# A spectral filter and an MLP mixer on one core: fixed places in the six channel pairs for the length-47 steps and the token quarters, and intermediate writes on SyncE's queue

## The chip, the core and the metric

The kernel runs on one core of one Trainium2 chip. The metric is the time of one execution in device microseconds (us); the median of several runs is quoted. A core has TensorE (PE: matmuls, with PEld for its weight loads), VectorE (DVE), ScalarE (ACT), GpSimd (POOL) and SyncE (SP), which here does nothing but issue transfers. All data are float32.

## The reference

```python
# x: (8, 3008, 256), filt_r and filt_i: (1505, 256)
X = np.fft.rfft(x, axis=1)
y = np.fft.irfft(X * (filt_r + 1j * filt_i)[None], n=3008, axis=1)
# the mixer on y: w_tok1 (3008, 256), w_tok2 (256, 3008), w_ch1 (256, 1536), w_ch2 (1536, 256)
yt = y.transpose(0, 2, 1)
h = np.maximum(yt @ w_tok1, 0.0) @ w_tok2
u = y + h.transpose(0, 2, 1)
out = u + np.maximum(u @ w_ch1, 0.0) @ w_ch2
```

## The kernel before

**The filter.** A sequence of 3008 = 47 x 64 is transformed in two stages. The steps **a** are the length-64 stage: one matmul of a sample's loaded rows (L472), a copy by ScalarE into a tile `t1` (L478, two buffers) and a write to a DRAM buffer `z` (L479), 12 a steps for a sample. The length-47 stage has 16 rounds c for a group of samples, each with three steps:

- **b** (`b_pair`): four pairs of matmuls into the two banks "acc" and "b" (L572), which VectorE then multiplies with the filter's rows into `p1` and `p2` (L583, two products of 128x1024 where the group has two samples)
- **m** (`join`): a subtraction and an addition on VectorE (L588, L589)
- **i** (`bi_pair`): matmuls into the same two banks (L572), two copies by ScalarE to `t3` (L561), and two writes to a DRAM buffer `g` (L598)

After b of round c, SP loads what round c+2 needs: two parts of `z` (L532), a table (L493) and eight pieces of the filter (L206, L208). Before the first b there is a step **w**, in which the first two rounds' loads are issued.

The samples stand in groups: (0), (1, 2), (3, 4), (5, 6), (7). Sample 0 is filtered ahead of everything. Each other group's filter runs in small steps beside the mixer of the group before it: samples 1 and 2 (the first transform here) beside the mixer of sample 0, 3 and 4 (the second) beside that of 1 and 2, 5 and 6 (the third) beside that of 3 and 4, and 7 (the fourth, half as wide) beside that of 5 and 6.

**The mixer.** The token product makes `u` in six tiles m of 512 columns (the last has 448) for each sample; the channel product goes through each tile in six **pairs** jp of hidden channels. Both products of the samples from 1 on use seven block products in place of eight, with sums on VectorE. A pair is issued in this order by `mix`, which hands over at three **places**:

- `up_first`: four matmul groups (L783) into two banks "pg", a copy `s` by ScalarE (L786), then on VectorE one `hh` and one `s` (L761). Then the sums `t` of the pair before (three pieces, L761) and the first part of `down` for the pair before (three groups, L817). *Place 0.*
- `up_last`: three groups (L799) into the same "pg" banks, two additions to `hh` on VectorE and two relus on ScalarE (L804). *Place 1.*
- the second part of `down` for the pair before (four groups, L817); in pair 0 this ends the tile before. *Place 2.*

`one_step` takes one piece of VectorE work from a list: after a tile's end those of `finish` (two at place 2 of pair 0, then one each at the next places: ten VectorE pieces, the last two being the transposes `turn`), after the next tile's `u` those of `u_sums` (a first piece, then two). Stores of a tile go out on POOL's queue (L864).

The next tile's `u` is made by `u_parts` at places that the table `own` gives. Sample 0 has two units (`u_unit`, L690 and L682). The other samples have four **quarters** (`u_quarter`, L704, quarters 2 and 3 also L682), each in one of the banks "acc" and "b", emptied by VectorE (quarter 0 by ScalarE and VectorE). After a quarter's last, SP loads the next token weights (`w2m_load`, L723). In pair 2 of a sample's last tile stand the next sample's token sums (L660, 96 matmuls). So a, b, i, the token units, the quarters and the token sums share two banks.

At every place the last loop looks whether the coming step of the filter is due there; only the order of instructions on each engine is set by this, and every engine works through its own in that order, held by semaphores. Before, for the groups from the second transform on:

```python
if coming in "aw":
    due = group == 0 or place == 1
elif group:
    due = (i % 2, place) == {"b": (1, 1), "m": (0, 0), "i": (0, 2)}[coming]
```

Of the kernel before, what the change touches and what calls it, by code (L numbers as in the profile page):

```python
# [27 lines left out]
KH = KR // 2  # L28
HALF = 64
XC = 2  # L30
# [5 lines left out]
KC = 2  # L36
# [5 lines left out]
JP = JT // 2  # L42
# [10 lines left out]
GROUPS = ((0,), (1, 2), (3, 4), (5, 6), (7,))  # L53
# [59 lines left out]
def kernel(  # L113
# [11 lines left out]
    nc = tc.nc  # L125
# [11 lines left out]
    place_of = {b: (g, i) for g, bs in enumerate(GROUPS) for i, b in enumerate(bs)}  # L137
    z_d, g_d = ([nc.dram_tensor("%s_tmp%d" % (what, g), (K2, KR, len(bs), D), FP32, kind="Internal").ap()
                 for g, bs in enumerate(GROUPS)] for what in "zg")
# [25 lines left out]
    def bank(tag):  # L165
        return (psg if tag == "pg" else psum).tile([P, 512], FP32, tag=tag, name="ps_" + tag)
# [5 lines left out]
    def free_bank():  # L172
        turn.reverse()
        return turn[0]
# [227 lines left out]
    def convert():  # L402

        convert_middle()
        convert_end()
# [60 lines left out]
    def rows_of(t_d, b):  # L466
        g, i = place_of[b]
        return t_d[g].rearrange("k (g a) b d -> (k g) a b d", a=A)[:, :, i, :]

    def a_unit(b, c):  # L470
        ps = bank(free_bank())
        nc.tensor.matmul(ps, wa0 if b == 0 else wa, xs.pop((b, c)).rearrange("p a d -> p (a d)"), start=True, stop=True)  # L472
        if b == 0:
            d0, c = divmod(c, NXC // 2)
            nc.scalar.copy(out=turned[:, ts(c, 2 * XC), ds(d0 * P, P)], in_=ps.rearrange("p (a d) -> p a d", d=P))
            return
        t1 = t1p.tile([P, XC, D], FP32, tag="t1", name="t1")
        nc.scalar.copy(out=t1.rearrange("p a d -> p (a d)"), in_=ps)  # L478
        nc.scalar.dma_start(rows_of(z_d, b)[:, ts(c, XC), :], t1)  # L479

    def dft(bs):
        first = bs[0] == 0
# [77 lines left out]
        def by_block(out, ps):  # L560
            nc.scalar.copy(out=out.rearrange("p b (e g i) -> p b g e i", e=DH, i=CW),  # L561
                           in_=ps.rearrange("p b (g e i) -> p b g e i", e=DH, i=CW))

        def two_banks():
            return [bank(tag).rearrange("p (b d) -> p b d", b=2)[:, 0:nb, :] for tag in turn]
# [3 lines left out]
        def four(outs, stat, mov):  # L569
            for i in range(2):  # L570
                for j in range(2):
                    nc.tensor.matmul(outs(i, j), stat(i, j), mov(i, j), start=True, stop=True)  # L572

        def both(half, n=HALF):
            return slice(half * HALF, half * HALF + n)
# [15 lines left out]
        def bi_pair(c):  # L591
            pss, wb, p = two_banks(), wbs[c], prods.pop((c, 0))
            four(lambda i, h: pss[i][both(h)], lambda i, h: wb[both(i), 2 + h], lambda i, h: p[both(i), h])
            t3 = t3p.tile([P, KC, nb, D], FP32, tag="t3", name="t3")
            for i in range(KC):
                by_block(t3[:, i], pss[i])
            for h in range(2):
                nc.scalar.dma_start(g_d[place_of[bs[0]][0]][ts(c, KC), ts(h, KH)].rearrange("k r b d -> r k b d"),  # L598
                                    t3[both(h, KH)])

        for c in range(FB):
# [49 lines left out]
    def t4_load(b, c, lo=PARTS[0], hi=P, queue=nc.sync):  # L651
        if lo == 0:
            t4[b, c] = t4p.tile([P, TC4, D], FP32, tag="t4", name="t4")
        queue.dma_start(t4[b, c][lo:hi], rows_of(g_d, b)[lo:hi, ts(c, TC4), :])
# [238 lines left out]
    def mix(next_ready):  # L893

        wait = []
        pos, hhs, tts = {}, {}, {}

        def loads(b):
            if b + 1 < B and next_ready(b):
                for c in wait:  # L900
                    t4_load(b + 1, c)
                wait.clear()


        own = ({(4, 0): (0,), (4, 2): (1,)}, {(3, 0): (0, 1), (4, 0): (2, 3)})
        new = {(JP - 2, 0): (0, 1), (JP - 1, 0): (2, 3)}

        def u_parts(b, m, jp, place):
            parts = own[b > 0] if m + 1 < MT else new if b + 1 < B else {}
            now = parts.get((jp, place), ())  # L910
            b, m = (b, m + 1) if m + 1 < MT else (b + 1, 0)
            for part in now:
                u_part(b, m, part)
            if now and now[-1] == max(p for ps in parts.values() for p in ps):
                if m:
                    wait.append(m)
                todo_v.extend(v_steps(b, m))
                if b and (b, m) < (B - 1, MT - 2):
                    w2m_load((m + 2) % MT)

        to_dram = [f for m in range(MT) for f in w2_sums(m)]
        items = [(b, m, jp) for b in range(B) for m in range(MT) for jp in range(JP)]
        n = MT * JP
        for i in range(len(items) + 1):
            now, old = i < len(items), i >= 1
            if ended[0] < len(tiles):
                convert()
            if now:
                b, m, jp = items[i]
                if i % n == 0:  # L930
                    wait.append(0)
                w = width(m)
                hhs[i] = hp.tile([P, 4, 256], FP32, tag="hh", name="hh")
                g = [bank("pg").rearrange("p (s n) -> p s n", s=2) for _ in range(2)]
                s = up_first(jp, uts[b, m], vts[b, m], w, g)
                up_middle(hhs[i], w, g, s)
            one_step()
            if old:
                bo, mo, jo = items[i - 1]
                tts[i - 1] = tp.tile([P, 4, 256], FP32, tag="t", name="t")  # L940
                for f in h_sums(hhs[i - 1], tts[i - 1], width(mo)):
                    f()
                down(mo, jo, 0, hhs[i - 1], tts[i - 1], pos.setdefault((bo, mo), []))
            if now:
                u_parts(b, m, jp, 0)
            yield b, i % n, 0
            if ended[0] < len(tiles):
                convert()
            if now:
                up_last(jp, uts[b, m], vts[b, m], w, g, s, hhs[i])  # L950
            one_step()
            loads(b)
            yield b, i % n, 1
            if old:
                down(mo, jo, 1, hhs.pop(i - 1), tts.pop(i - 1), pos[bo, mo])
                if jo == JP - 1:
                    todo_v.extend(finish(bo, mo, uts[bo, mo], pos[bo, mo]))
                    one_step()
                    one_step()
            if now:  # L960
                if b + 1 < B and i % n == n - 4:
                    h1s[b + 1] = token_relu(b + 1, token_sums(b + 1))
                u_parts(b, m, jp, 2)
                if jp == JP - 1:
                    while todo_v and m + 1 == MT:
                        one_step()
                if i >= 8 and to_dram:
                    to_dram.pop(0)()
                if i in (28, 29):
                    w2m_load(i - 28)  # L970
            loads(b)
            yield b, i % n, 2
        while todo_v:
            one_step()

    with tc.manual_schedule():
# [6 lines left out]
        for i, _ in enumerate(dft(GROUPS[0])):  # L983
            if i == 0:
                nc.scalar.dma_start(wai_t, wait_d)
            k = i - NXC - 2
# [50 lines left out]
        group, todo, done = -1, iter(()), True  # L1037

        def next_ready(b):
            return done or b != GROUPS[group][-1]  # L1040
# [3 lines left out]
        coming = "a"  # L1044
        for b, i, place in mix(next_ready):
            if group + 1 < len(GROUPS) and b == GROUPS[group + 1][0]:
                if not done:
                    raise AssertionError("the filter's steps don't fit beside the mixer's")
                group += 1
                done = group + 1 == len(GROUPS)  # L1050
                todo = iter(()) if done else dft(GROUPS[group + 1]) if group else second
                coming = "a"
            if done:
                continue
            if coming in "aw":
                due = group == 0 or place == 1
            elif group:
                due = (i % 2, place) == {"b": (1, 1), "m": (0, 0), "i": (0, 2)}[coming]
            elif i < 27:
                due = (i % 3, place) in {"b": ((2, 1), (0, 2)), "m": ((0, 0), (1, 1)), "i": ((0, 1), (2, 0))}[coming]  # L1060
            else:
                due = place == {"b": 2, "m": 0, "i": 1}[coming]
            if due:
                coming = next(todo, "end")
                done = coming == "end"
# [30 lines left out]
```

## Time and profile before

| | |
|---|---|
| median of three runs | 2552.43 us (2550.9 to 2552.93) |
| the profiled execution's own time | 2553.45 us |
| its span, first to last instruction | 2551.7 us |
| granted TensorE clock, mean | 0.993 |
| busy: PE, PEld, DVE | 2444.5, 1984.0, 1811.3 us |
| busy: ACT, POOL | 675.5, 595.5 us |
| moved by DMA | 235.96 MB, 92 GB/s over the span |

The difference between an execution's time and its span is what lies before the first and after the last instruction. A line of the profile's groups or of the order of time names the engine, the line in the kernel, the operation and the tiles written and read; an "issue" or "q" behind an engine's name (SPq, ACTq) is its own queue of instructions, which issues transfers. Matmuls are pipelined, and their ends in the trace are modelled, so what a matmul costs is read from start to start.

### The profile page before, as it was taken

What the parts mean: (1) busy time and instruction counts of PE and PEld (TensorE: products, weight loads), DVE (VectorE), ACT (ScalarE), POOL (GpSimd) and SP (SyncE); (2) the same over time, 40 slices, a digit from 0 to 9 for tenths busy, and PEclk for the clock granted to TensorE, in tenths of its full rate; (3) what the DMA queues carried; (4) which work ended last, traced back from release to release, by engine and by line L of the source; (5) the groups of instructions that cost most, each with busy time, mean ns of one, the idle gap of its engine ahead of it and who ended that gap; (6) DMA issues with size and microseconds to landing.
All of it is one profiled execution on the core that took longest, in us unless ns stands there. A gap on an engine that the chain in (4) does not pass through costs nothing.

```text
span 2551.7 us, 33219 instructions
## 1 busy us (share of the span) xinstructions
PE 2444.5 (96%) x11716; PEld 1984.0 (78%) x11716; DVE 1811.3 (71%) x3344; ACT 675.5 (26%) x1348; POOL 595.5 (23%) x1086
## 2 busy tenths in 40 slices
PE   6889999999999999999999999999999999999997
PEld 3556666788877777888887777798888888898887
DVE  6686777576685887756775788757778577757776
ACT  4633222123221222222222222212222122212221
POOL 6573332112111121221121111211211121211222
PEclk8999999999999999999999999999999999999999
DMA  9974444243342333224333333314232222101100
GB/s 202 242 217 127 115 123 139 72 127 107 101 107 65 89 98 80 69 76 124 95 96 80 91 93 80 85 31 127 87 99 78 57 61 71 55 25 30 42 14 19
DMA packets 172478, 235.96 MB, mean 92 GB/s; under 512 B 32386, under 2 KB 122742, under 8 KB 172312
## 3 DMA queue, kind: packets, MB, share of 16 engines
q1 hardware_dynamic: 98728, 137.77, 19.3%
q0 software_dynamic: 33376, 48.46, 7.7%
q10 hardware_dynamic: 40208, 47.61, 6.4%
q8 instruction: 93, 1.52, 0.3%
q14 instruction: 73, 0.60, 0.1%
HBM read 156.49 MB, written 77.22 MB: 92 GB/s over the span
## 4 chain that ended last, share of the span: by engine, by line
PE 74%; DVE 13%; DMA 5%; ACT 3%; issue 3%; ACTq 1%; POOL 0%; DVEq 0%; SPq 0%; POOLq 0%
PE ps_po L817 27%; PE ps_pg L783 15%; PE ps_pg L799 11%; PE ps_b L660 3%; PE ps_acc L660 3%; DVE t L761 3%; PE ps_b L572 3%; PE ps_acc L704 3%; DVE hh L761 2%; PE ps_b L704 2%; DVE p L583 2%; DVE s L761 2%; PE ps_b L682 2%; PE ps_acc L682 2%; PE ps_b L472 1%
## 5 line engine op out<-in xcount | busy, mean ns | idle before, releaser
L761 DVE TENSOR_TENSOR hh<-ps_pg,s 128x512 f32<-128x512 f32 (+3 forms) x864 | 483.0, 587 | 493.2 <-ACT s L786 481.6
L864 POOL DMA_DIRECT2D out_dram<-r x757 | 410.5, 551 | 1679.2 <-ACT hh L804 805.3
L804 ACT ACTIVATE hh<-hh 128x512 f32<-128x512 f32 (+1 forms) x576 | 347.5, 621 | 1204.7 <-DVE hh L761 1204.7
L817 PE MATMUL ps_po<-t,wc 128*128 128x256 f32 (+1 forms) x2304 | 546.6, 380 | 12.8 <-DVE t L761 11.6
L817 PEld LDWEIGHTS ps_po<-t,wc 128*128 128x128 f32 x2304 | 429.7, 190 | 146.8 <-issue 42.9
L783 PE MATMUL ps_pg<-v,wc 128*128 128x256 f32 (+1 forms) x1728 | 415.3, 376 | 2.2 <-DVE v L761 2.1
L817 PE MATMUL ps_po<-hh,wc 128*128 128x256 f32 (+1 forms) x1728 | 414.1, 376 | 0.4 <-DVE r L761 0.2
L783 PEld LDWEIGHTS ps_pg<-v,wc 128*128 128x128 f32 x1728 | 328.7, 191 | 42.8 <-DVE v L761 4.8
L817 PEld LDWEIGHTS ps_po<-hh,wc 128*128 128x128 f32 x1728 | 329.3, 191 | 38.8 <-DVE r L761 0.6
L799 PE MATMUL ps_pg<-u,wc 128*128 128x256 f32 (+1 forms) x1152 | 294.2, 378 | 14.2 <-DVE hh L761 14.1
L799 PEld LDWEIGHTS ps_pg<-u,wc 128*128 128x128 f32 x1152 | 214.9, 190 | 56.5 <-DVE hh L761 26.0
L761 DVE TENSOR_TENSOR t<-t,hh 128x256 f32<-128x256 f32 (+1 forms) x576 | 243.7, 423 | 19.8
L761 DVE TENSOR_TENSOR s<-ps_pg,hh 128x512 f32<-128x512 f32 (+1 forms) x288 | 196.1, 681 | 30.3 <-DVE hh L761 0.5
L761 DVE TENSOR_TENSOR t<-hh 128x512 f32<-128x512 f32 (+1 forms) x288 | 192.6, 669 | 0.6 <-ACT hh L804 0.6
L783 PE MATMUL ps_pg<-u,wc 128*128 128x256 f32 (+1 forms) x576 | 175.9, 387 | 9.4 <-DVE hh L761 9.4
L786 ACT COPY s<-ps_pg 128x256 f32<-128x256 f32 (+1 forms) x288 | 105.9, 368 | 248.8 <-PE ps_pg L783 238.6
L799 PE MATMUL ps_pg<-v,wc 128*128 128x256 f32 (+1 forms) x576 | 168.7, 375 | 0.0
L783 PEld LDWEIGHTS ps_pg<-u,wc 128*128 128x128 f32 x576 | 104.7, 191 | 63.9 <-DVE hh L761 30.8
L799 PEld LDWEIGHTS ps_pg<-v,wc 128*128 128x128 f32 x576 | 108.6, 190 | 13.2
L583 DVE TENSOR_TENSOR p<-ps_b,filt 128x1024 f32<-128x1024 f32 (+1 forms) x64 | 69.4, 1084 | 24.3 <-PE ps_acc L572 20.0
L761 DVE TENSOR_TENSOR u<-ps_acc,u 128x512 f32<-128x512 f32 (+2 forms) x108 | 62.4, 578 | 31.8 <-PE ps_acc L704 27.1
L660 PE MATMUL ps_b<-t,w 128*128 128x256 f32 x384 | 83.6, 379 | 0.7 <-issue 0.7
(135 smaller groups left out, 2420.0 us busy)
## 6 DMA issues: line engine op xcount, KB each, us to landing
w<-w_tmp SPq DMA_DIRECT2D x35, 896.0 KB
out_dram<-r POOLq DMA_DIRECT2D x698, 32.0 KB, 1.8
g_tmp<-t ACTq DMA_DIRECT2D x112, 192.0 KB
z_tmp<-t ACTq DMA_DIRECT2D x84, 256.0 KB
t<-g_tmp SPq DMA_DIRECT2D x42, 512.0 KB
filt<-in_x_dram SPq DMA_DIRECT2D x145, 128.0 KB
t<-z_tmp SPq DMA_DIRECT2D x96, 192.0 KB
wb<-wbi_t SPq DMA_DIRECT2D x64, 128.0 KB
```

Source lines behind the costliest of these rows:

```text
L572: nc.tensor.matmul(outs(i, j), stat(i, j), mov(i, j), start=True, stop=True)
L583: nc.vector.tensor_tensor(out=prods[c, h], in0=pss[h].unsqueeze(1).to_broadcast([P, 2, nb, D]), in1=filts[c % FB][:, :, 0, :].unsqueeze(2) ...
L660: nc.tensor.matmul(acc[:, t, :], w1[:, a, ts(t, P)], t4[b, a // TC4][:, a % TC4, :], start=(a == 0 and t == 0), stop=(a == A - 1 and t == ...
L682: nc.tensor.matmul(ps[:, ds(q * P, n)], t4[b, c][:, r, ts(dh, P)], wai[:, 0:n], start=(first and q == 0), stop=(not first and q == 3))
L704: nc.tensor.matmul(ps[:, ds(j * hw, hw)], h1[:, n, :], w2m[m % 2][:, at, 0:hw], start=(i < 2 and j == 0), stop=(j == len(todo) - 1))
L761: nc.vector.tensor_tensor(out=out, in0=in0, in1=in1, op=op)
L783: nc.tensor.matmul(ps[:, 0:hw], chan[0][:, jp, n, :], mov, start=True, stop=True)
L786: nc.scalar.copy(out=s[:, 0], in_=g[0][:, 0, 0:hw])
L799: nc.tensor.matmul(ps[:, 0:hw], chan[0][:, jp, n, :], mov, start=True, stop=True)
L804: nc.scalar.activation(out=hs, in_=hs, func=AF.Relu)
L817: nc.tensor.matmul(po[i][:, j, 0:hw], chan[1][:, jp, n, :], mov, start=(jp == 0 and first == 1), stop=(jp == JP - 1 and last == 1))
L864: q.dma_start(bass.AP(tensor=ob.tensor, offset=ob.offset + row * D + g * cw, ap=[[N1 * D, 32], [D if h else -D, n], [1, cw]]), blocks[ts(g ...
```

## The change

- From the second transform on, b, m and i get fixed places in the six pairs of a tile, two rounds in a tile: b at place 1 of pairs 5 and 2, m at place 0 of pairs 0 and 3, i at place 0 of pair 1 and place 2 of pair 3. Before, a round began in every second pair, so three in a tile.
- In the first transform, b stands at place 1, m at place 2 and i at place 0 of the next pair; rounds begin in pairs 5, 1, 2 and 3, from tile 4 on in pair 0 too.
- From the second transform on, a and w steps come at places 1 and 2 of a pair, not at place 1 alone.
- The quarters 0 to 3 stand at place 0 of pair 3, place 0 of pair 4, and place 2 of pair 4 (two), not in two twos at place 0 of pairs 3 and 4. Sample 0's two units stand both at place 2 of pair 4, not one at place 0. For a sample's first tile (`new`) nothing is changed.
- The writes of `g` in `bi_pair`, and those of `z` from samples 3 on, are issued by SyncE, not by ScalarE.

```diff
@@ a_unit
-        nc.scalar.dma_start(rows_of(z_d, b)[:, ts(c, XC), :], t1)
+        (nc.scalar if b in GROUPS[1] else nc.sync).dma_start(rows_of(z_d, b)[:, ts(c, XC), :], t1)
@@ bi_pair
-                nc.scalar.dma_start(g_d[place_of[bs[0]][0]][ts(c, KC), ts(h, KH)].rearrange("k r b d -> r k b d"),
+                nc.sync.dma_start(g_d[place_of[bs[0]][0]][ts(c, KC), ts(h, KH)].rearrange("k r b d -> r k b d"),
                                     t3[both(h, KH)])
@@ mix
-        own = ({(4, 0): (0,), (4, 2): (1,)}, {(3, 0): (0, 1), (4, 0): (2, 3)})
+        own = ({(4, 2): (0, 1)}, {(3, 0): (0,), (4, 0): (1,), (4, 2): (2, 3)})
         new = {(JP - 2, 0): (0, 1), (JP - 1, 0): (2, 3)}
@@ the last loop
+            jp = i % JP
             if coming in "aw":
-                due = group == 0 or place == 1
+                due = group == 0 or place > 0
             elif group:
-                due = (i % 2, place) == {"b": (1, 1), "m": (0, 0), "i": (0, 2)}[coming]
-            elif i < 27:
-                due = (i % 3, place) in {"b": ((2, 1), (0, 2)), "m": ((0, 0), (1, 1)), "i": ((0, 1), (2, 0))}[coming]
+                due = (jp, place) in {"b": ((5, 1), (2, 1)), "m": ((0, 0), (3, 0)), "i": ((1, 0), (3, 2))}[coming]
             else:
-                due = place == {"b": 2, "m": 0, "i": 1}[coming]
+                due = (jp - (coming == "i")) % JP in ((5, 1, 2, 3) if i < 4 * JP else (5, 0, 1, 2, 3)) and place == {"b": 1, "m": 2, "i": 0}[coming]
```

## The prediction

> **What bounds the kernel now.** First the page's busy line and its chain of waits:
>
> ```profile
> PE 2444.5 (96%) x11716; PEld 1984.0 (78%) x11716; DVE 1811.3 (71%) x3344; ACT 675.5 (26%) x1348; POOL 595.5 (23%) x1086
> ...
> PE 74%; DVE 13%; DMA 5%; ACT 3%; issue 3%; ACTq 1%; POOL 0%; DVEq 0%; SPq 0%; POOLq 0%
> ```
>
> TensorE looks full, yet the chain gives it only 74% and VectorE 13%: some of the 96% is matmuls standing in line. So I compared one tile (six channel pairs) with and without the filter's steps in it, by a table of stretches: 336-392 is sample 0 beside the first transform, 866-918 sample 2 beside the second, 2155-2197 sample 6 with nothing beside it.
>
> ```profile
> 336.10:391.90 55.80, 52.82 (x258) 36.37 (x257) 42.65 (x72) 15.06 (x29) 16.36 (x28) 1.00 0.41 113
> 866.40:917.70 51.30, 49.36 (x248) 37.12 (x247) 41.82 (x73) 13.21 (x27) 8.66 (x16) 1.00 0.36 93
> 2155.20:2196.70 41.50, 41.38 (x200) 36.27 (x200) 31.70 (x61) 10.31 (x21) 8.66 (x16) 1.00 0.16 49
> ```
>
> After the length come PE, PEld, DVE, ACT, POOL. Three transform steps c (each b, m, i) cost 51.3 - 41.5 = 9.8 us, 3.3 each; weight loads fill 72% of the middle tile and 87% of the last. Then the order of time, pair 3 of that tile, on TensorE:
>
> ```profile
> 889.66 0.70 PE L783 MATMUL ps_pg<-u,wc 128*128 128x256 f32 x2
> 890.20 1.46 PE L783 MATMUL ps_pg<-v,wc 128*128 128x256 f32 x6
> 891.49 1.46 PE L817 MATMUL ps_po<-hh,wc 128*128 128x256 f32 x6
> 892.79 1.03 PE L704 MATMUL ps_acc<-w 128*128 128x256 f32 x4
> 893.65 1.03 PE L704 MATMUL ps_b<-w 128*128 128x256 f32 x4
> 894.52 1.03 PE L799 MATMUL ps_pg<-u,wc 128*128 128x256 f32 x4
> 895.38 0.59 PE L799 MATMUL ps_pg<-v,wc 128*128 128x256 f32 x2
> 897.12 0.65 PE L572 MATMUL ps_b<-t,wb 48*64 48x512 f32 x2 [1.15 <-issue]
> ```
>
> and on ScalarE and VectorE:
>
> ```profile
> 890.37 0.57 ACT L561 COPY t<-ps_b 128x512 f32<-128x512 f32 x1
> 890.83 0.59 ACT L561 COPY t<-ps_acc 128x512 f32<-128x512 f32 x1
> 891.45 0.79 ACTq L598 DMA_DIRECT2D g_tmp<-t  x2
> 892.29 0.37 ACT L786 COPY s<-ps_pg 128x256 f32<-128x256 f32 x1 [0.86 <-PE ps_pg L783]
> ...
> 892.69 0.43 DVE L761 TENSOR_TENSOR hh<-ps_pg,s 128x256 f32<-128x256 f32 x1 [2.28 <-ACT s L786]
> 895.87 1.15 DVE L761 TENSOR_TENSOR u<-ps_b,u 128x512 f32<-128x512 f32 x2
> 898.24 1.23 DVE L583 TENSOR_TENSOR p<-ps_b,filt 128x1024 f32<-128x1024 f32 x1
> ```
>
> Read it so: the i step's two copies and its two writes hold ScalarE until 892.24, the copy s comes late, VectorE idles 2.28 us for it and then empties the two quarters' banks only at 897.02; b, which needs those banks, starts at 897.12 instead of 895.81. That is 1.3 us of TensorE, in each of the tiles.
>
> **What the Trainium skill says.** "Perfetto Trace Analysis", Identifying the Most-Contended Engine: matmul busy share is no measure of TensorE's headroom, weight-load share is better; the trace agrees (PE busy 96% and 99.7% in the last two stretches, weight loads 72% and 87%). "TensorE: Matmul & The Clock Gate", Architectural detail: ACT and DVE are strict first in, first out; the late copy above is that. "DMA: Bandwidth & Descriptors", Issuing engines are not separate DMA queues: issuing elsewhere saves only the issuer's time; that time is 0.79 us of ScalarE per c here, and no row here shows what these writes' landing becomes on SP's queue.
>
> **Prices.** Start to start on TensorE: up_first 1.73, down's two parts 1.30 and 1.73, up_last 1.30, so a bare pair is 6.04. A b or i step is 1.02 and makes the next group 0.1 longer: 1.12. Quarters: 0.87, 0.87, 1.76, 1.32. An a step 0.86. Start to start on VectorE: hh 0.53, s 0.61, t 0.72 + 0.46 + 0.34, two hh from L799's banks 0.60 each, a product of b 1.13 (two), m's two 0.60 each, finish's ten pieces 0.3 to 0.7 each. ScalarE: copy s can start 1.1 after its pair starts.
>
> **Second and third transform (samples 3-4, 5-6), step by step.** Before, the pairs of the 866 tile start at 866.4, 873.5, 881.5, 889.7, 900.1, 910.3, 917.7: 7.1, 8.0, 8.2, 10.4, 10.2, 7.4. Afterwards a tile carries two c, not three:
> - Pair 0, m at place 0: nothing more on TensorE. VectorE still owes 1.7 us of products from pair 5; they end before copy s matters. 6.2.
> - Pair 1, i at place 0: 7.16 and 0.4 late, because finish's sums and m sit before the next hh on VectorE. 7.6. (Bare, this pair already stalls 0.36; i covers part.)
> - Pair 2, b at place 1: up_last's hh end near 6.0, turn 6.6, products 8.9; the next hh isn't due until 7.3 + 1.5. 7.3.
> - Pair 3, quarter 0, m, i at place 2: m ends at 6.0, i comes at 7.0. 6.04 + 0.87 + 1.12 = 8.0; 8.1.
> - Pair 4, quarter 1 at place 0, quarters 2, 3 at place 2: the i copies end at 1.3, with no writes behind them copy s starts then; its banks are free when quarter 1 comes at 3.1. 6.04 + 0.1 + 0.87 + 3.08 = 10.1.
> - Pair 5, b: now v's first sums fall at place 0 and the other two (0.9) in front of the products. They end at 6.9; the next up_first needs them at 7.3 + 0.4. 7.3.
>
> Sum 46.6, minus 41.5 bare: 5.1 for two c, 2.5 each against 3.3. Whole transform: samples 1+2 took 603 us and 3+4 607 (516.3 to 1119.4 to 1726.9). Bare samples would take 2 x 265 (five tiles of 41.4 or a little less, the last with its 20.7 us of token sums 58.4); 24 a steps add 19; so 54 and 58 us are the 16 c. Afterwards 16 x 2.5 = 40, and 3.5 for the crossing into the next sample (the b there stays in front of v's last sums: pair 0 starts with a 1.2 us wait in both) and for token sums behind b's products: 43.5. **Gain 10.5 + 14.5 = 25 us.** The fourth (sample 7 alone, half as wide; 29.6 us by the same sum, 1.85 per c, of which 1.38 is TensorE's own) gains less: 1.55 x 16 = 25. **4.5 us.**
>
> **First transform (samples 1-2 beside sample 0).** From 239.2 to 469.6, 230.4 us; the same 24 pairs bare are 166, so 4.0 per c against 2.24 of TensorE's own. Before, m and i follow b so closely that up_last or i waits for products. Afterwards b, m at places 1, 2 and i at place 0 of the next pair: from b to i lie 4.9 us of TensorE work, VectorE needs 2.3 + 1.2 for products and m. A pair with one whole c is 8.3 on TensorE and 7.3 on VectorE, so it runs at 8.3 unless finish's pieces (pairs 0-2) intrude: I get 7.3, 7.3, 8.9, 8.7, 12.5 (both token units at place 2), 7.3: 51.9 for the tile that took 55.8. All: 35.7 (rest of tile 1) + 51.9 + 51.9 + 54.6 (tile 4, five c, pair 1 waits 1 us for m) + 13.2, and 3 us at the start, where filter rows land late: 210. **Gain 20 us.**
>
> **Costed at nothing.** a steps twice a pair: 0.86 each as before, banks alternate, and each copy (0.59) fits between ScalarE's relus and copy s. Their x loads: six in flight, two used per 7.8 us. From the last a to the first b 14 us instead of 21; the filter rows' issue ends about 9 after it: 3 to 5 are left for landing. Token quarters alone (no transform beside): v's last sum lands about when up_first's second matmul is due; 0 to 0.1 per tile, 2 at most. Writes on SP: 128 of g (0.79 per two), 60 of z (0.37). A g write waits for i's copies, about 1.3 after i; behind it stand the loads of c+3, which wait for b of c+1 anyway, 2.4 after i. SP's densest stretch, 11 loads in 4.9 us per c, becomes 5.7 per 8.3. Lower bound 0 or a gain (ScalarE no longer waits in its issues, which reach 1.47 us); upper bound in the second rival. Token-sum loads of the next sample follow the last g write with over 15 us to spare.
>
> **Sum.** 25 + 4.5 + 20 = 49, minus 2 for quarters: 47. Profiled execution 2553.45 (span 2551.7 and 1.75 around it), median of three 2552.43, 0.04% apart: 2552.4 - 47 = **2505 us**.
>
> **Rivals.**
> 1. VectorE stays the gate (0.25): v's sums before the products in pair 5 and finish behind m in pair 0 delay pairs 0 and 1 by 1.5 us per tile more than I sum, and the first transform gets half. For it: VectorE is 82% busy in the 866 tile. Against: two c per tile take 3.5 us off it. 47 - 16 - 10: 2531.
> 2. SP holds ScalarE (0.08), slower: z's buffers are two, so a step i+2's copy waits until write i has landed. If SP reaches the write late, ScalarE stands, copy s behind it, TensorE behind that one for one. Copy to copy is 7.8 us; 0.6 copy, 0.4 issue, 1.8 to 4.6 landing (bounds: stores and w_tmp writes) use 3 to 5.6; it decides once SP is over 2 to 5 us late. SP does wait up to 64 us for w2_tmp loads, but for quarters that TensorE passes before the a step. At 1 us in each of 60: 2505 + 60 = 2565.
> 3. The first transform is bound by landing, not order (0.10): filter rows already came 4 us or more after issue near 245. No gain there, 2525.
>
> My forecast has 0.57, 2490 to 2520 for itself. Taking 0.2% as what a measurement here tells from no change: faster 0.89, same 0.03 (the far ends of rivals 1 and 3), slower 0.08. Range 2480 to 2538, which takes in rivals 1 and 3.
>
> **What would show it.** Tiles of samples 2 and 4 near 46.6 with two c; 336-392's counterpart near 52 with four; no gap before L572 in pair 3; no ACTq row in the L598 line; copy s at 1.1 to 1.3. Wrong: tiles of 48 or more, waits of ACT on DMA at z's copies, or L583 waiting for filter loads.

## The result and the profile after

| | before | after |
|---|---|---|
| median of four runs each | 2552.68 us (2550.9 to 2553.71) | 2508.71 us (2507.99 to 2509.31) |
| ratio, 95% interval | | 0.9828 (0.9811 to 0.9845) |
| the profiled execution, its span | 2553.45, 2551.7 us | 2507.99, 2506.2 us |

The change is worth 44.0 us of the 47 that were forecast, and 2508.7 lies in the range. First the page of after, its busy line and the shares of its chain of waits:

```profile
PE 2434.7 (97%) x11716; PEld 1982.6 (79%) x11716; DVE 1811.4 (72%) x3344; ACT 681.6 (27%) x1348; POOL 601.2 (24%) x1086
...
PE 82%; DVE 12%; issue 2%; DMA 2%; ACT 1%; DVEq 0%; SPq 0%; ACTq 0%; POOL 0%; POOLq 0%
```

Busy times hardly move: the same work is done. TensorE's share of the chain goes from 74% to 82%; ScalarE with its queue falls from 4% to 1%. Then the table of stretches, for a tile of sample 2 with steps, one of sample 0 beside the first transform, and a bare one of sample 7 (length, then PE, PEld, DVE, ACT, POOL):

```profile
849.30:895.90 46.60, 46.38 (x232) 36.71 (x231) 38.24 (x69) 12.28 (x24) 8.71 (x16) 1.00 0.31 80
327.20:379.50 52.30, 52.20 (x258) 36.80 (x258) 42.72 (x70) 14.96 (x29) 17.09 (x28) 1.00 0.45 121
2333.10:2374.60 41.50, 41.38 (x200) 36.20 (x199) 31.53 (x62) 10.23 (x21) 8.69 (x16) 1.00 0.12 32
```

The tile of sample 2 now takes 46.6 us, but it holds two rounds c and not three; the tile of sample 0 takes 52.3 for the same four that took 55.8. Pair 3 of the first of these, in the order of time on TensorE and on ScalarE:

```profile
870.51 0.59 PE L783 MATMUL ps_pg<-u,wc 128*128 128x256 f32 x2
870.94 1.46 PE L783 MATMUL ps_pg<-v,wc 128*128 128x256 f32 x6
872.23 1.46 PE L817 MATMUL ps_po<-hh,wc 128*128 128x256 f32 x6
873.53 1.03 PE L704 MATMUL ps_acc<-w 128*128 128x256 f32 x4
874.39 1.03 PE L799 MATMUL ps_pg<-u,wc 128*128 128x256 f32 x4
```

```profile
871.62 0.37 ACT L786 COPY s<-ps_pg 128x256 f32<-128x256 f32 x1 [1.66 <-PE ps_pg L783]
```

Copy s starts 1.1 us after the pair (870.51 to 871.62), where it was 2.6; there is one quarter in place of two, no write on ScalarE's queue, and no gap.

Where the time of the two profiled executions lies, by the starts of pairs on TensorE (us; a second profile of each kernel in brackets, see below):

| stretch | before | after | predicted change | measured |
|---|---|---|---|---|
| ahead of sample 0's first pair | 150.6 (147.9) | 143.4 (143.2) | 0 | -7.2 (-4.7) |
| a steps of samples 1 and 2 | 88.5 (87.9) | 90.1 (90.1) | 0 | +1.6 (+2.3) |
| first transform | 230.4 (234.6) | 215.8 (212.6) | -20 | -14.6 (-22.0) |
| samples 1 and 2 | 603.1 (603.0) | 594.3 (594.3) | -10.5 | -8.8 (-8.7) |
| samples 3 and 4 | 607.5 (609.5) | 594.0 (594.0) | -14.5 | -13.5 (-15.5) |
| samples 5 and 6 | 569.2 (569.2) | 566.0 (566.0) | -4.5 | -3.3 (-3.3) |
| sample 7 | 242.4 (242.4) | 242.7 (242.7) | part of +2 | +0.3 (+0.4) |

The last three transforms repeat within 0.1 us from profile to profile, but for samples 3 and 4 of the kernel before; the head and the first transform do not. The granted TensorE clock is part of that: each trace has some stretches, most of 3.4 us, in which it was half (0.51 from 1451.9 to 1455.3 in the kernel before, in samples 3 and 4). By the traces' clock, an estimate of the time lost so in the first transform is 1.7 us before (5.1 in its second profile) and 1.7 after (0), in samples 3 and 4 before 1.7 (3.4); samples 1 to 6 of the kernel after have no such stretch. So below, parts are weighed by the time of **samples 1 to 6 together** (1779.8 us before, 1754.2 after) and of the first transform, with the medians beside them.

### The profile page after: what moved, and what is told of

Same layout as the page of the kernel before. It is cut to its first block, busy times and chain, and to the rows that moved or that the text cites. A ratio compares the mean times of both kernels' runs of the same rounds, so it can differ in the third digit from the quotient of the medians.

```text
span 2506.2 us, 33323 instructions
## 1 busy us (share of the span) xinstructions
PE 2434.7 (97%) x11716; PEld 1982.6 (79%) x11716; DVE 1811.4 (72%) x3344; ACT 681.6 (27%) x1348; POOL 601.2 (24%) x1086
## 4 chain that ended last, share of the span: by engine, by line
PE 82%; DVE 12%; issue 2%; DMA 2%; ACT 1%; DVEq 0%; SPq 0%; ACTq 0%; POOL 0%; POOLq 0%
PE ps_po L817 29%; PE ps_pg L783 17%; PE ps_pg L799 12%; PE ps_b L660 3%; PE ps_acc L660 3%; PE ps_b L572 3%; DVE t L761 3%; PE ps_b L704 3%; PE ps_acc L704 2%; DVE p L583 2%; DVE hh L761 2%; PE ps_b L682 2%; PE ps_acc L682 2%; DVE s L761 1%; PE ps_b L472 1%
## 5 line engine op out<-in xcount | busy, mean ns | idle before, releaser
L799 PEld LDWEIGHTS ps_pg<-u,wc 128*128 128x128 f32 x1152 | 215.3, 190 | 63.0 <-DVE hh L761 29.0
L783 PE MATMUL ps_pg<-u,wc 128*128 128x256 f32 (+1 forms) x576 | 173.9, 384 | 13.5 <-DVE hh L761 13.5
L761 DVE TENSOR_TENSOR u<-ps_b,u 128x512 f32<-128x512 f32 (+3 forms) x107 | 61.7, 577 | 69.7 <-PE ps_b L704 65.0
L761 DVE TENSOR_TENSOR u<-ps_acc,u 128x512 f32<-128x512 f32 (+3 forms) x103 | 58.9, 572 | 57.2 <-PE ps_acc L704 52.0
L660 PE MATMUL ps_b<-t,w 128*128 128x256 f32 x384 | 83.9, 380 | 5.3 <-DVE p L583 4.7
```

The costliest lines, as they stand in the source:

```text
L660: nc.tensor.matmul(acc[:, t, :], w1[:, a, ts(t, P)], t4[b, a // TC4][:, a % TC4, :], start=(a == 0 and t == 0), stop=(a == A - 1 and t == ...
L761: nc.vector.tensor_tensor(out=out, in0=in0, in1=in1, op=op)
L783: nc.tensor.matmul(ps[:, 0:hw], chan[0][:, jp, n, :], mov, start=True, stop=True)
L799: nc.tensor.matmul(ps[:, 0:hw], chan[0][:, jp, n, :], mov, start=True, stop=True)
```

## Experiments

The theory to test was the prediction's: the new places carry the gain, since TensorE had waited for VectorE's work in the wrong order, and the writes on SP come along for little. The rival: ScalarE's writes were what made the old tiles long. The runs of this part are compared with 1779.8 us for samples 1 to 6 before, of which up to 1.7 are the half clock.

**The two halves of the change, each alone.** Places and quarters of after, writes back on ScalarE:

```diff
-        (nc.scalar if b in GROUPS[1] else nc.sync).dma_start(rows_of(z_d, b)...
+        nc.scalar.dma_start(rows_of(z_d, b)...
-                nc.sync.dma_start(g_d...
+                nc.scalar.dma_start(g_d...
```

> The places alone: the kernel after with the writes of z and g issued by ScalarE again, so 0.982 of the time before becomes what the places and quarters are worth by themselves. Theory (the places carry the gain, the writes only remove a stall of 0.7 us in pair 3 of tiles with a c): 2511 to 2520 us, that is 3 to 12 us above the kernel after; tiles of samples 2 and 4 at 46.6 to 47.2 us, the first transform's tile at 52 to 53, and a stall on ScalarE's queue ahead of some copy s again. Rival (ScalarE's issues were what made the tiles long, the places only came along): 2530 us or more, tiles of sample 2 near 49. The 7.2 us that went ahead of sample 0's first pair and that no edit touches: if they go with the writes, the first pair starts near 150.6 us here; if they are the chance of this program's transfers, it may start anywhere from 143 to 151.

And the kernel before with only those two lines changed the other way:

> The writes alone: the kernel before with z's and g's writes on SyncE's queue, its places as they were. Theory: pair 3 of a tile with c loses its stall of some 0.7 us, and the irregular waits for ScalarE go; 24 tiles of such a kind by 0.3 to 0.5 us give 7 to 12 us: 2540 to 2546 us; the tiles of three c stay near 49, the first transform's near 55. Rival (ScalarE's issues made the tiles long): 2520 us or less. Third (VectorE is the gate with the old places whatever ScalarE does): no change, 2550 to 2553. The start of sample 0's first pair: near 143.4 us if the 7.2 us go with the writes, else near 150.6.

| | median, us | ratio (95%) | first transform | samples 1 to 6 |
|---|---|---|---|---|
| places alone | 2511.69 | 0.9841 (0.9827 to 0.9856) | 212.5 | 1758.1 (-21.7) |
| writes alone | 2518.51 | 0.9864 (0.9847 to 0.9880) | 226.3 | 1749.9 (-29.9) |
| both (after) | 2508.71 | 0.9828 (0.9811 to 0.9845) | 215.8 | 1754.2 (-25.6) |

The first expectation held. The second failed, and its rival (2520 us or less) held: the writes alone bring 33 us and not 7 to 12, three quarters of the whole, and in samples 1 to 6 they bring *more* than both together. The two halves are worth 40 and 33 us and together 44: some 29 us are the same microseconds, taken twice. The tile of sample 2 shows them. Times from pair to pair on TensorE:

| pair | before | writes alone | places alone | after | predicted for after |
|---|---|---|---|---|---|
| 0 | 7.16 | 7.16 | 6.43 | 6.43 | 6.2 |
| 1 | 7.99 | 7.36 | 7.53 | 7.53 | 7.6 |
| 2 | 8.16 | 7.67 | 7.26 | 7.26 | 7.3 |
| 3 | 10.42 | 9.45 | 8.02 | 8.02 | 8.1 |
| 4 | 10.24 | 10.24 | 10.09 | 10.09 | 10.1 |
| 5 | 7.37 | 7.36 | 7.26 | 7.26 | 7.3 |
| tile | 51.3 | 49.2 | 46.6 | 46.6 | 46.6 |
| rounds c, us for each above the bare 41.4 | 3: 3.3 | 3: 2.6 | 2: 2.6 | 2: 2.6 | 2: 2.5 |

With the writes alone, pairs 1, 2 and 3 get 0.6, 0.5 and 1.0 us shorter, 2.1 a tile. Pair 3 of that run on ScalarE, and the end of its TensorE part:

```profile
884.50 0.57 ACT L561 COPY t<-ps_b 128x512 f32<-128x512 f32 x1
884.97 0.59 ACT L561 COPY t<-ps_acc 128x512 f32<-128x512 f32 x1
885.44 0.39 ACT L786 COPY s<-ps_pg 128x256 f32<-128x256 f32 x1
```

```profile
889.52 0.59 PE L799 MATMUL ps_pg<-v,wc 128*128 128x256 f32 x2
890.29 0.65 PE L572 MATMUL ps_b<-t,wb 48*64 48x512 f32 x2 [0.18 <-PE ps_pg L799]
```

The pair started at 883.80. Copy s follows i's copies at once, 1.6 us in and not 2.6, and of the 1.3 us that b waited 0.34 are left (890.29 against 889.95, two matmul spacings of 0.216 after 889.52). Pair 1 has the same cause: in the kernel before the i step's writes stood ahead of its copy s too:

```profile
875.43 0.80 ACTq L598 DMA_DIRECT2D g_tmp<-t  x2
876.28 0.37 ACT L786 COPY s<-ps_pg 128x256 f32<-128x256 f32 x1 [0.88 <-PE ps_pg L783]
```

Pair 2 has no write ahead of its copy s; it pays for pair 1's lateness: b's products reach VectorE 0.3 us after the pair's start before (881.81 against 881.50), and 0.2 us ahead of it with the writes moved (875.94 against 876.13).

With the places alone these rows are still there, in pair 1 and ahead of pair 4's copy s:

```profile
863.32 0.79 ACTq L598 DMA_DIRECT2D g_tmp<-t  x2
865.01 1.23 ACT L804 ACTIVATE hh<-hh 128x512 f32<-128x512 f32 x2 [1.72 <-DVE hh L761]
...
881.92 0.79 ACTq L598 DMA_DIRECT2D g_tmp<-t  x2
882.75 0.37 ACT L786 COPY s<-ps_pg 128x256 f32<-128x256 f32 x1 [0.86 <-PE ps_pg L783]
```

In pair 1, i now comes behind copy s, and its writes are out 0.9 us before the relus' input is there (864.11 against 865.01). In pair 4 the same 0.79 us of issues stand between i's copies and copy s; but there a quarter comes between `down` and `up_last`, and TensorE returns to the "pg" banks after they are read. (The old pair 3 had two quarters there; what was late in it was b, which wants the quarters' own banks straight after `up_last`. In these tiles b now stands in no pair with a quarter.) So one half takes the writes out of ScalarE's queue, the other puts them where TensorE has something else to do: **two remedies for one stall**.

**Which of the writes.** The kernel before, g's writes alone on SP (the second line of the diff, not the first):

> The kernel before with only g's writes on SyncE's queue; z's stay on ScalarE's. Theory (a g write holds ScalarE's queue in front of the next pair's copy s; z's writes fall where ScalarE has time): as with both writes moved, 2515 to 2523 us, tiles of sample 2 at 49.2 us, samples 1 to 6 together near 1750 us. Rival (z's writes matter too): 2530 us or more, and samples 3 and 4, whose mixer carries the first z writes that move, longer than with both moved by 3 us or more.

Measured: 2519.26 us, ratio 0.9870 (0.9854 to 0.9886), tiles of sample 2 at 49.25, samples 1 to 6 at 1752.1. g's writes give 27.7 of the 29.9 us; z's the other 2.3, spread over all samples (samples 3 and 4: 593.0 against 592.2). The theory holds.

**The suspected cost doubled.** The kernel before with each write of g in two halves:

```diff
+            parts = 1 if first else 2
             for h in range(2):
+                for n in range(parts):
-                nc.scalar.dma_start(g_d[...][ts(c, KC), ts(h, KH)]..., t3[both(h, KH)])
+                    nc.scalar.dma_start(g_d[...][ts(c, KC), ds(h * KH + n * KH // parts, KH // parts)]...,
+                                        t3[ds(h * HALF + n * KH // parts, KH // parts)])
```

> The suspected cost doubled: the kernel before with every round's two writes of g, still on ScalarE's queue, cut into four of half the size (the same bytes; sample 0's own filter stays as it was). Theory (ScalarE stands 0.4 us in every issue, and copy s behind it): 0.8 us more ahead of copy s in the pairs that follow an i step; two or three of three rounds in a tile pay it, so 1.6 to 2.4 us a tile of three rounds and 16 rounds in each of three transforms: 2572 to 2590 us, tiles of sample 2 at 53 to 54 instead of 51.3. Rival (VectorE's order makes the old tile long, ScalarE is covered): no change, 2549 to 2556 us. Rival (the landing of the bytes counts, not the issues): no change either, tiles at 51.3.

Measured: 2599.61 us, ratio 1.0194 (1.0171 to 1.0217). The direction is the theory's, both rivals fall, but the cost is 47 us and not 20 to 38. Pair 3 of sample 2's tile m1 on ScalarE (lines below the edit are two higher here):

```profile
899.93 1.76 ACTq L600 DMA_DIRECT2D g_tmp<-t  x4
901.74 0.37 ACT L788 COPY s<-ps_pg 128x256 f32<-128x256 f32 x1 [1.83 <-DMA g_tmp<-t]
```

Four writes of half the size take 1.76 us of ScalarE where two took 0.79: an issue costs by the piece, not by the byte. Then b on TensorE in pair 3 of this tile and of the next, m2, and the stretches of the two pairs (length, PE, PEld, DVE, ACT, POOL, then the granted clock):

```profile
906.57 0.89 PE L572 MATMUL ps_b<-t,wb 48*64 48x512 f32 x2 [2.11 <-issue]
...
962.04 0.65 PE L572 MATMUL ps_b<-t,wb 48*64 48x512 f32 x2 [2.12 <-issue]
```

```profile
898.15:911.17 13.02, 10.91 (x47) 7.85 (x45) 8.31 (x14) 3.72 (x8) 8.69 (x16) 0.87 0.41 101
953.62:965.00 11.38, 9.27 (x47) 7.21 (x45) 7.80 (x14) 3.73 (x8) 8.68 (x16) 1.00 0.37 90
```

In both tiles b starts 8.42 us after its pair, where it was 7.46 (897.12 against 889.66): 0.96 us later for 0.97 us more of issuing, one for one, while up_last starts as early as before. Pair 3 of m2 grows by just that, from 10.42 to 11.39; pairs 1 and 5, which had been covered in part, by 0.8 and 0.7: 2.5 us for the tile (53.8), as the theory had it. Pair 3 of m1 takes 13.03 us, because the clock was half for 3.4 us from 906.8 on and b and `down` ran slow. Samples 1 to 6 take 42.6 us more; in them the clock was half for 23.9 us, against 3.4 in the kernel before. Half of that difference, 10 us, is an estimate of the clock's part, which leaves 32 for the issuing. All four executions of this kernel have a lower mean clock (0.984 to 0.989) than the seven of the kernel before beside them (0.991 or 0.992), so the clock's part comes along with the edit; why is not shown.

**The same doubling beside the new places.**

> The doubled writes beside the new places: places and quarters of the kernel after, g's and z's writes on ScalarE, every round's two writes of g cut into four of half the size. With the places alone copy s of pair 4 starts 2.05 us after its pair and s is read by 3.7, while TensorE comes back to those banks at 3.9, after the quarter that stands there. Theory (the new places hide ScalarE's issues behind other TensorE work, up to that 0.2 us of slack): 0.9 us more of issuing gives 0.5 to 0.8 us in pair 4, nothing in pair 1, so tiles of sample 2 at 47.1 to 47.4 us and 2516 to 2530 us, against 48 us that the same doubling cost with the old places. Rival (the places hide nothing, they only carry fewer rounds in a tile): 2.5 to 4 us for three rounds as before, so 1.7 to 2.7 for two, tiles at 48.3 or more, 2545 us or more.

Measured: 2517.53 us, ratio 0.9874 (0.9857 to 0.9892), sample 2's tiles m1 and m2 at 46.9 and 46.6; samples 1 to 6 take 1761.5 us, 3.5 more than with two writes. Pair 4 stays at 10.09, so its cover is larger than the 0.2 us that I had read. The same doubling costs 42.6 us with the old places (some 32 without the clock's part) and 3.5 with the new ones: that shows that the places hide ScalarE's issues.

**The first transform's places alone.** The kernel after with the old rule and the old quarters from the second transform on, the writes on SP:

> The first transform's places alone: the kernel after with the old places and old quarters from the second transform on; writes on SyncE, the first transform's steps and quarters as in the kernel after. Theory (gains add: 14.6 us in the first transform, 8.8 + 13.5 + 3.3 us in samples 1 to 6): the loss against the kernel after is 25.6 us less what the writes give to samples 1 to 6 alone, 0 to 8 us: 2526 to 2535 us, samples 1 and 2 at 600 us together, 3 and 4 at 602 to 607. Rival (later samples gain by the writes, not by the places): 2512 us or less. The start of sample 0's first pair is near 143.4 us if it goes with the writes or the program's head, which are those of the kernel after.

Measured: 2504.58 us, ratio 0.9821 (0.9800 to 0.9842); first transform 215.3, samples 1 to 6 at 1749.7. The theory (2526 or more) fails and the rival holds: with the writes on SP, the old order of the later transforms is as good as the new.

**The quarters put back.** The kernel after with the old quarters:

```diff
-        own = (..., {(3, 0): (0,), (4, 0): (1,), (4, 2): (2, 3)})
+        own = (..., {(3, 0): (0, 1), (4, 0): (2, 3)})
```

> The quarters alone put back: the kernel after with the token product's four quarters in pairs 3 and 4 by twos, as before, the steps' places and the writes as after. Theory (pair 3 of a tile with steps has m's adds at the same place in every second c, so two quarters there make VectorE late by some 0.6 us; bare tiles gain the 0.08 us that pair 0 now takes more): 24 tiles with steps by 0.2 to 0.4 us of loss, 24 bare ones by 0.08 of gain: 2510 to 2517 us. Rival (the quarters' move is a cost that the places carried along): faster than the kernel after by 2 to 4 us, 2505 to 2507 us.

Measured: 2503.75 us, ratio 0.9812 (0.9797 to 0.9828); samples 1 to 6 at 1749.1. The rival holds: the quarters' move *costs* 5.1 us there and 0.3 in sample 7. A tile with steps is 46.28 against 46.59, all of it in pair 0 (6.12 against 6.43). VectorE ahead of that pair, in after:

```profile
894.60 0.88 DVE L761 TENSOR_TENSOR v<-v,u 128x256 f32<-128x256 f32 x2
895.45 1.23 DVE L583 TENSOR_TENSOR p<-ps_b,filt 128x1024 f32<-128x1024 f32 x1
896.59 1.22 DVE L583 TENSOR_TENSOR p<-ps_acc,filt 128x1024 f32<-128x1024 f32 x1
897.72 0.41 DVE L761 TENSOR_TENSOR hh<-ps_pg,s 128x256 f32<-128x256 f32 x1
```

and with the old quarters:

```profile
895.53 1.22 DVE L583 TENSOR_TENSOR p<-ps_b,filt 128x1024 f32<-128x1024 f32 x1
896.66 1.22 DVE L583 TENSOR_TENSOR p<-ps_acc,filt 128x1024 f32<-128x1024 f32 x1
898.14 0.42 DVE L761 TENSOR_TENSOR hh<-ps_pg,s 128x256 f32<-128x256 f32 x1 [0.27 <-ACT s L786]
```

A quarter that comes later makes v's last sums late, and they then stand ahead of b's products. VectorE reaches pair 0's hh without a pause and 0.3 us late (1.8 us after the pair's start, against 1.5), where with the old quarters it waits 0.27 us for copy s. This run and the one before it differ only in the later transforms' places: 1749.1 against 1749.7. Beside the writes on SP **those places are worth 0.6 us**.

**The head.** It was 7.2 us shorter after, with nothing of the change in it, so both kernels were profiled again unchanged:

> The kernel before, unchanged, profiled again, for the stretch ahead of sample 0's first pair (150.6 us before, 143.4 after, 146.6 to 153.0 in the runs with parts of the change). If that stretch varies from execution to execution, it ends away from 150.6 by a microsecond or more; if it belongs to the program, within half a microsecond of it. All later stages as before within 0.5 us.

> The kernel after, unchanged, profiled again, for the same stretch: 143.4 us within half a microsecond if it belongs to the program, a microsecond or more away if it varies from execution to execution. All later stages as after within 0.5 us.

The head took 147.9 us (before; 2556.19 us in all) and 143.2 (after; 2504.68). So it moves by 2.7 us from one execution of the same program to another. Over all runs it lies between 143.2 and 153.0: 146.6 with the places alone, 153.0 with both writes on SP, 145.5 with g's alone, which is no order by any part of the change. What sets it in an execution stays open. Two later stretches missed the half microsecond as well: the first transform (234.6 against 230.4 before, 212.6 against 215.8 after), and samples 3 and 4 of the kernel before (609.5 against 607.5). There the half clock accounts for 3.4 of the 4.2 us, 1.7 of the 3.2 and 1.7 of the 2.0, by the estimate above.

**Two versions that build on this.** In after, TensorE also waits in pair 2 of sample 1's last tile, for b's products (on TensorE; L660 are the token sums):

```profile
754.52 1.78 PE L817 MATMUL ps_po<-t,wc 128*128 128x224 f32 x8
758.09 4.15 PE L660 MATMUL ps_b<-t,w 128*128 128x256 f32 x18 [1.79 <-DVE p L583]
```

The token sums need the banks that the products read, and begin when the second product ends, at 758.04. With the old quarters, and b one pair later in that tile:

```diff
-  ... {"b": ((5, 1), (2, 1)), "m": ((0, 0), (3, 0)), "i": ((1, 0), (3, 2))}
+  last = i >= (MT - 1) * JP
+  ... {"b": ((5, 1), (3 if last else 2, 1)), "m": ((0, 0), (4 if last else 3, 0)), "i": ((1, 0), (4 if last else 3, 2))}
```

> A version that may beat both: the kernel after with the old quarters, and in a sample's last tile b at place 1 of pair 3, m at place 0 and i at place 2 of pair 4, in place of pairs 2 and 3, so that b's products no longer stand in front of the token sums' additions on VectorE in pair 2. Theory: the 2.0 us that TensorE waits there go, three times, and 0.3 us come back at the quarters of pair 4: 2497 to 2501 us, the tiles b1 m5 and b3 m5 at 63.6 instead of 65.35. Rival (VectorE is only late elsewhere, at pair 4's quarters or at pair 5's products): no change from 2503.8 us, those tiles at 65 or more.

Measured: 2500.51 us, ratio 0.9800 (0.9781 to 0.9818), the two tiles at 63.23 instead of 65.35, samples 1 to 6 at 1743.6, 5.5 less than with the old quarters alone. The theory holds, and the 0.3 us did not come back. Then also b at place 2 of pair 5 in that tile (`(5, 2 if last else 1)`), so that v's sums go first:

> The version with old quarters and b at place 1 of pair 3 in a sample's last tile, with b at place 2 instead of place 1 of pair 5 there, so that v's last sums stand ahead of b's products on VectorE. Theory: the wait of 1.2 us of TensorE at the start of the next sample's pair 0 goes, three times, and at most half of it comes back because the products then delay that pair's hh: 1.5 to 3.5 us off 2500.5, so 2497 to 2499 us; tile b1 m5 together with b2 m0 at 109.4 to 109.8 us instead of 110.4. Rival (the products delay pair 0's hh and so up_last by as much as they delayed the sums): no change, 110.2 or more.

Measured: 2497.63 us, ratio 0.9787 (0.9772 to 0.9801), the fastest kernel here. But b1 m5 with b2 m0 takes 109.9 us, between the theory's 109.4 to 109.8 and the rival's 110.2: of the wait at the crossing 1.07 us go from up_first, and 0.74 come back at the end of pair 0, where pair 1's up_first waits for `hh`, which stands behind the products. Samples 1 to 6 win 1.7 us; of the 4.4 us between the two profiled spans (2493.4 and 2497.8) 3.4 lie in the first transform, which the edit does not touch (up to 1.7 of them by a half clock that only the slower one has).

## Why the prediction was right, and where its steps were not

- **Second to fourth transform, by pairs: right as a picture of the new kernel.** Of the six pairs of the tile 6.2, 7.6, 7.3, 8.1, 10.1, 7.3 none is off by more than 0.23 us, and the sum is exact. The gains of 10.5, 14.5 and 4.5 were 8.8, 13.5 and 3.3. Of the 4 us by which the prediction let samples 3 and 4 cost more than 1 and 2 ("54 and 58 us are the 16 c"), up to 1.7 were the half clock at 1451.9 and no step. Its sum 25 + 4.5 + 20 is 49.5, not 49.
- **The cause it gave: wrong in part.** It read pair 3 rightly ("the i step's two copies and its two writes hold ScalarE"), gave no cause for the length of pairs 1 and 2 of the old tile, and put the writes on SP under "Costed at nothing", "Lower bound 0 or a gain". With the old places that gain is 29.9 us of samples 1 to 6; with the new ones, which had already hidden it, 3.9 (1758.1 to 1754.2). So to count it as nothing was nearly right beside the new places only, and the sum came out; but "2.5 each against 3.3" did not need them. The runs: 3.3 to 2.6 by the writes alone, 3.3 to 2.6 by the places alone, 2.4 ((46.28 - 41.43) / 2) with both and the old quarters.
- **First transform: right in cause, its gain smaller.** Predicted 210 us and 20 gained; 215.8 and 212.6 in two profiles of after, 14.6 and 22.0 gained. Less the estimated time of the half clock it is 228.7 and 229.5 before, 214.1 and 212.6 after: 15 to 17 gained. Its tile is 52.2 for the 51.9 foreseen. Here the places do carry it: 212.5 with them alone, 226.3 (222.9 less the half clock) with the writes alone.
- **Quarters: mis-sized.** "0 to 0.1 per tile, 2 at most" holds for a bare tile (41.51 against 41.43) but not with steps, where it is 0.31; 5.4 us in all. The prediction saw the sums in front of the products, and said of the products that "they end before copy s matters": they end 1.9 us after pair 0's start, copy s after 1.5.
- **Sample 0's units beside a steps: left out.** The prediction has both units at place 2 of pair 4 for the tiles with rounds, but nothing for sample 0's first tile, which carries a steps. Its pair 4 takes 15.72 us instead of 13.94, in both profiles of each kernel: the first unit had stood where TensorE now waits, in the second profile of after:

```profile
199.13 1.13 PE L799 MATMUL ps_pg<-u,wc 128*128 128x256 f32 x4 [1.49 <-DVE hh L761]
```

  These 1.8 us are the main part of the 1.6 to 2.3 by which the stretch of the a steps got longer; the a steps there are placed as before.
- **The head** was not foreseen and is no effect of the change that these runs show: -7.2 us in the first pair of profiles. There it makes up for most of the 8.7 us by which the other stages fall short of 47, and so far the agreement of that pair is luck; in the second pair the other stages fall short by 0.2.
- **Rivals.** VectorE as the gate (2531) and the landing of filter rows (2525) did not come, though b's first products did wait in tile 1. SP holding ScalarE (2565) did not come either. The longest wait of a z copy beside sample 1 looks like it, in tile 0 (TensorE, then ScalarE):

```profile
537.85 1.02 PE L472 MATMUL ps_b<-filt,wa 128*128 128x512 f32 x2
```

```profile
538.95 0.59 ACT L478 COPY t<-ps_b 128x512 f32<-128x512 f32 x1 [4.29 <-issue]
539.82 0.37 ACT L786 COPY s<-ps_pg 128x256 f32<-128x256 f32 x1 [0.29 <-PE ps_pg L783]
```

  But the copy's own matmul ends only at 538.87: the copy waits for that, and starts 0.08 us later. The buffer's last write had been issued at 528.46, ten us earlier. No z copy beside the samples from 1 on waits for a write to land, and copy s starts 1.1 us after its pair (538.7), as it should. With the old places the z writes on SP gained 2.3 us.

The Trainium skill, "DMA: Bandwidth & Descriptors", Issuing engines are not separate DMA queues, says that issuing elsewhere saves the issuer's time; the runs agree, with a size: 0.79 us of ScalarE for each c, of which the old places exposed most (2.1 of 2.4 us in a tile of three). The prediction cited it and then priced that time at nothing.

## What to carry to other kernels

If an engine that works in order issues a transfer ahead of a short operation on which others wait, the time of the issue can come out on the critical path, with the old places here one for one (0.96 us of b for 0.97 of issuing). Look for issue rows directly ahead of such an operation in *every* period of the loop, and price moving them to an idle engine by itself, ahead of any reordering. When two edits of one change can cure the same wait, their gains don't add; run each alone before crediting either, and look at what the bundle carries along, for here one part (the quarters) cost 5 us.

## What the runs showed of the hardware that was not expected

- Issuing is paid by the piece: two writes of 192 KB took 0.79 us of ScalarE, four of 96 KB 1.76 us. 0.97 us more of issuing ahead of one copy made b 0.96 us later.
- The granted clock halves for stretches of 3.4 us, and one such stretch can fall into a single pair: of two tiles with the same instructions and the same wait of 2.1 us, pair 3 took 13.03 us where the mean clock was 0.87, and 11.39 where it was 1.00. A pair that is out of line with its counterpart should be read beside the clock before a mechanism is sought.
- The head of the same program took 150.6 and 147.9 us in two executions and the first transform 230.4 and 234.6, while the last three transforms, samples 3 and 4 before excepted, repeated within 0.1 us: parts of a change of some microseconds are told apart by stages, not by the total.
